# Batch 0's first x tiles normalised in pairs by head halves, and another order of block 0's first units

## The chip, the cores and the metric

The kernel runs on one core of one Trainium2 chip. The metric is the device time of one execution in microseconds, the lower the better; the median of several runs is quoted. Engines are named as in the profile: PE (TensorE, matmuls and transposes), PEld (its weight loads), DVE (VectorE), ACT (ScalarE), POOL (GpSimd), SP (SyncE, which here issues DMAs).

## What is computed

A linear attention ("cosformer") of 8 batches, 8 heads, 576 positions and head width 64, followed by a gated feed-forward block over all 4608 tokens:

```python
def phi(x, c, s):
    r = np.maximum(x, 0.0)
    return np.concatenate([r * c, r * s], axis=-1)     # 64 -> 128 features
q_p = phi(q, cos_w, sin_w); k_p = phi(k, cos_w, sin_w)
kv  = np.einsum('bhsf,bhsd->bhfd', k_p, v)
z   = np.sum(k_p, axis=2)
num = np.einsum('bhsf,bhfd->bhsd', q_p, kv)
den = np.einsum('bhsf,bhf->bhs', q_p, z)[..., None] + 1e-06
x   = (num / den)            # transposed and reshaped to (4608, 512)
out = (gelu(x @ w_gate) * (x @ w_val)) @ w_out         # 512 -> 1536 -> 512
```

Inputs and the output are float32; the matmuls take bfloat16. In the kernel gelu is the activation function of ACT.

## The kernel before

**Tiles.** A batch's 576 positions are held as four tiles of 128 and one of 64. The features are 128 per head, so `kp` and `qp` hold, for each tile `j` and head, 64 cosine and 64 sine columns; `sk` and `sq` scale k and q into them (one instruction for the cosine half and one for the sine half, `"v"` for DVE and `"s"` for ACT; a pair of last arguments restricts it to some heads). `cast_v` turns v into bfloat16 with a column of ones beside it, so that the matmul that gives kv gives z as well. `kv_half(b, g, ...)` makes kv of four heads (group g) in one PSUM bank, 20 matmuls, and `kv_evac` copies it to SBUF. `q_by_pe` turns a q tile by eight PE transposes into a bank, and `q_evac` copies it into `qT`. `numer_mm(b, t, bank, g)` makes numerators and denominators of tile t and group g in bank `bank + g`; `norm` takes the reciprocal of den and multiplies (three DVE instructions) into `xb`; `x_by_pe` turns that by four PE transposes, one for each 128 channels, and copies them into `xT`, which the feed-forward block reads. `numer` is both groups of `numer_mm` and one `norm` over both.

**Feed-forward block.** The hidden width 1536 is cut into 12 tiles `jt`. `gate(n, jt, c0, w, gb)` is four matmuls into bank `gb` for `w` token columns from `c0` of block n, and a gelu by ACT into one of four `gel` buffers. `value` is four matmuls into another bank and, by DVE, the product with `gel` into `hT`. `gv_unit` is a gate and its value. Block 0 has 576 columns, the later ones 512.

**Order.** The kernel fixes the order of every engine's instructions by the order of the program text (`tc.manual_schedule()`); each engine runs its own list in that order and waits on semaphores for what the other engines make. At the start k, q and v of batch 0 come by DMA from SP's and ACT's queues, v in two halves of heads; the weights come by POOL's queue, the first of them (`load_w(0, 2)`) behind a copy by ACT that reads q, the last of batch 0 (`load_w(8, 12)`) behind a small POOL copy that reads x of tile 0, so that the loads follow each other. `dummies(n)` are matmuls whose result nobody reads. q of batch 1 and the weights `wo` follow on POOL behind the last scales of q; k and v of batch 1 wait for the first part of `wo`.

Block 0's first units are written out by hand. As soon as the x^T columns of tile t are there (128 columns, 64 for tile 4), gates and values over these columns can run. In the text before, tile 0's columns are used by weight tiles 0 and 1, then tile 1's, then weight tiles 2 and 3 over both (`A`, 256 columns), and so on; `X(t, bank, eng)` stands for the transposes and copy of tile t, `Y(t, bank)` for its numerators and norm. From weight tile 4's second part on (`Bw`, 320 columns) a loop carries on, then the blocks follow; the change does not touch them.

Of the kernel before, what the change touches and what calls it, by code (L numbers as in the profile page):

```python
# [9 lines left out]
FP32 = mybir.dt.float32  # L10
BF16 = mybir.dt.bfloat16
AF = mybir.ActivationFunctionType
ALU = mybir.AluOpType
# [3 lines left out]
def kernel(  # L17
# [10 lines left out]
    nc = tc.nc  # L28

    B, H, S, D = q.shape  # L30
# [4 lines left out]
    CT = C // 128  # L35
    JT = J // 128
    NJ = 4
    EPS = 1e-6
# [11 lines left out]
    rot = ctx.enter_context(tc.tile_pool(name="rot", bufs=2))  # L50
    pp = ctx.enter_context(tc.tile_pool(name="pp", bufs=1, space=bass.MemoryType.PSUM))

    ps = pp.tile([128, 8, 512], FP32, name="ps")
# [15 lines left out]
    hT = [sb.tile([128, JT, 64 + 576], BF16, name=f"hT{i}") for i in range(2)]  # L69

    junk = hT[1][:, 0, 0:512]
    ident = sb.tile([128, 128], BF16, name="ident")
    tiny = sb.tile([1, 8], FP32, name="tiny")

# [50 lines left out]
    def dummies(n, bank=7):  # L125
        for _ in range(n):
            nc.tensor.matmul(ps[:, bank, :], lhsT=junk[:, 0:128], rhs=junk, start=True, stop=True)  # L127
# [20 lines left out]
        )  # L148


    def kv_half(b, g, bank, eng="s"):
        for h in range(4 * g, 4 * g + 4):
            for j in range(NJ + 1):
                nc.tensor.matmul(  # L154
                    ps[:, bank, (h % 4) * (D + 1):(h % 4 + 1) * (D + 1)],
                    lhsT=kp[:, j, h, :],
                    rhs=vx[b % 2][:, j, h, 0:D + 1],
                    start=(j == 0), stop=(j == NJ),
                )
        if eng is not None:  # L160
            kv_evac(b, g, bank, eng)

    def kv_evac(b, g, bank, eng):
        src = ps[:, bank, 0:4 * (D + 1)].rearrange("p (h e) -> p h e", e=D + 1)
        dst = kv[b % 2][:, 4 * g:4 * g + 4, 0:D + 1]
        (nc.scalar.copy if eng == "s" else nc.vector.tensor_copy)(dst, src)

    def numer_mm(b, t, bank, g, rows=128):
        for h in range(4 * g, 4 * g + 4):
            nc.tensor.matmul(  # L170
                ps[0:rows, bank + g, (h % 4) * (D + 1):(h % 4 + 1) * (D + 1)],
                lhsT=qT[b % 2][:, t, h, 0:rows],
                rhs=kv[b % 2][:, h, 0:D + 1],
                start=True, stop=True,
            )

    def norm(xb, bank, g0, g1, rows=128):

        n = g1 - g0
        nd = ps[0:rows, bank + g0:bank + g1, 0:4 * (D + 1)].rearrange("p g (h e) -> p g h e", e=D + 1)  # L180
        den = rot.tile([128, 2, 4], FP32, name="den")
        nc.vector.tensor_scalar(den[0:rows, 0:n], nd[:, :, :, D], EPS, None, op0=ALU.add)  # L182
        rec = rot.tile([128, 2, 4], FP32, name="rec")
        nc.vector.reciprocal(rec[0:rows, 0:n], den[0:rows, 0:n])
        nc.vector.tensor_tensor(  # L185
            xb[0:rows, g0:g1], nd[:, :, :, 0:D],
            rec[0:rows, 0:n, :, None].to_broadcast([rows, n, 4, D]), op=ALU.mult,
        )

    def new_xb():  # L190
        return rot.tile([128, 2, 4, D], BF16, name="xb", bufs=4)

# [21 lines left out]
    def gate(n, jt, c0, w, gb):  # L214

        p0 = starts[n] + c0
        for ct in range(CT):
            nc.tensor.matmul(  # L218
                ps[:, gb, 0:w], lhsT=wg_sb[:, ct, jt * 128:(jt + 1) * 128],
                rhs=xT[:, ct, p0:p0 + w], start=(ct == 0), stop=(ct == CT - 1),  # L220
            )
        gels[n, jt, c0] = gel = rot.tile([128, 512], FP32, name="gel", bufs=4)
        nc.scalar.activation(gel[:, 0:w], ps[:, gb, 0:w], AF.Gelu)  # L223

    def value(n, jt, c0, w, vb):

        p0 = starts[n] + c0
        for ct in range(CT):
            nc.tensor.matmul(  # L229
                ps[:, vb, 0:w], lhsT=wv_sb[:, ct, jt * 128:(jt + 1) * 128],  # L230
                rhs=xT[:, ct, p0:p0 + w], start=(ct == 0), stop=(ct == CT - 1),
            )
        gel = gels.pop((n, jt, c0))
        nc.vector.tensor_mul(hT[n % 2][:, jt, 64 + c0:64 + c0 + w], gel[:, 0:w], ps[:, vb, 0:w])  # L234

    def gv_unit(n, jt, c0, w, gb, vb, mid=()):
        gate(n, jt, c0, w, gb)
        for f in mid:
            f()
        value(n, jt, c0, w, vb)  # L240
# [79 lines left out]
    def q_by_pe(b, j, bank, eng, h0=0, h1=H):  # L320

        qb = ps[:, bank, :].bitcast(BF16).rearrange("p (h t) -> p h t", h=H)
        for h in range(h0, h1):
            nc.tensor.transpose(out=qb[:, h, :], in_=qp[:, j, h, :], identity=ident)  # L324
        if eng is not None:
            q_evac(b, j, bank, eng, h0, h1)

    def q_evac(b, j, bank, eng, h0=0, h1=H):
        qb = ps[:, bank, :].bitcast(BF16).rearrange("p (h t) -> p h t", h=H)
        cp = nc.vector.tensor_copy if eng == "v" else nc.scalar.copy  # L330
        if j < NJ:
            cp(qT[b % 2][:, j, h0:h1], qb[:, h0:h1])
        else:
            cp(qT[b % 2][:, j, h0:h1, 0:64], qb[:, h0:h1, 0:128:2])

    def x_by_pe(b, t, xb, bank, eng, c0=0, c1=CT):
        p0 = b * S + t * 128
        cp = nc.vector.tensor_copy if eng == "v" else nc.scalar.copy
        xb2 = xb.rearrange("p g h d -> p (g h d)")
        rows = 128 if t < NJ else 64  # L340
        view = ps[:, bank, 0:256].bitcast(BF16).rearrange("p (c t) -> p c t", c=CT)
        for ct in range(c0, c1):
            nc.tensor.transpose(  # L343
                out=view[:, ct, 0:rows], in_=xb2[0:rows, ct * 128:(ct + 1) * 128], identity=ident[0:rows, 0:rows],
            )
        cp(xT[:, c0:c1, p0:p0 + rows], view[:, c0:c1, 0:rows])  # L346

    def sq(j, which, eng, *h):
        scale(Q, j, which, eng, *h)

    def sk(j, which, eng, *h):
        scale(K, j, which, eng, *h)
# [3 lines left out]
    for h0 in (0, 4):  # L356
        for j in range(NJ + 1):
            sk(j, 0, "v", h0, h0 + 4)
            sk(j, 1, "v" if j < 2 else "s", h0, h0 + 4)
    nc.scalar.copy(wg_sb[0:2, 0, 0:1], qf[0:2, 7, 1, D - 1:D])  # L360
    load_w(0, 2)
    load_w(2, 4)
    load_w(4, 8)
    for j in range(2):
        sq(j, 0, "v"), sq(j, 1, "s")
        q_by_pe(0, j, j, None)
    dummies(3)
    q_evac(0, 0, 0, "v")
    cast_v(0, 0, 2, "v")
    cast_v(0, 2, 4, "s")  # L370
    kv_half(0, 0, 4, None)
    q_evac(0, 1, 1, "v")
    dummies(2)
    cast_v(0, 4, 6, "v")
    cast_v(0, 6, 8, "s")
    kv_evac(0, 0, 4, "v")
    kv_half(0, 1, 5, "s")
    x0, x1 = new_xb(), new_xb()
    numer_mm(0, 0, 6, 0)
    norm(x0, 6, 0, 1)  # L380
    dummies(1, 4)
    numer_mm(0, 0, 6, 1)
    sq(2, 1, "s")
    norm(x0, 6, 1, 2)
    sq(2, 0, "v")
    numer_mm(0, 1, 0, 0)
    numer_mm(0, 1, 0, 1)
    norm(x1, 0, 0, 2)
    x_by_pe(0, 0, x0, 4, "s", 0, 2)
    dummies(2, 5)  # L390
    x_by_pe(0, 0, x0, 4, "s", 2, 4)
    q_by_pe(0, 2, 3, None)

    nc.gpsimd.tensor_copy(tiny[0:1, 1:2], x0[0:1, 1, 3, D - 1:D])
    load_w(8, 12)


    A, Bw = (0, 256), (256, 320)
    xs = {1: x1}

    def X(t, bank, eng):
        return lambda: x_by_pe(0, t, xs[t], bank, eng)

    def Y(t, bank):
        def f():
            xs[t] = numer(0, t, bank, 128 if t < NJ else 64)
        return f

    gate(0, 0, 0, 128, 5)
    gate(0, 1, 0, 128, 4)  # L410
    X(1, 2, "s")()
    q_evac(0, 2, 3, "v")
    sq(3, 0, "v"), sq(3, 1, "s")
    value(0, 0, 0, 128, 6)
    value(0, 1, 0, 128, 7)
    Y(2, 0)()
    gate(0, 0, 128, 128, 5)
    gate(0, 1, 128, 128, 4)
    value(0, 0, 128, 128, 2)
    value(0, 1, 128, 128, 3)  # L420
    q_by_pe(0, 3, 6, "s")
    gate(0, 2, *A, 5)
    X(2, 0, "v")()
    sq(4, 1, "s"), sq(4, 0, "v")
    gate(0, 3, *A, 4)
    value(0, 2, *A, 7)
    Y(3, 0)()
    value(0, 3, *A, 2)
    q_by_pe(0, 4, 3, "s")
    gv_unit(0, 0, 256, 128, 5, 6)  # L430
    gv_unit(0, 1, 256, 128, 4, 7, (X(3, 0, "s"),))
    Y(4, 2)()
    gv_unit(0, 0, 384, 128, 5, 1)
    gv_unit(0, 1, 384, 128, 4, 0)
    gate(0, 4, *A, 5)
    X(4, 7, "v")()
    gate(0, 5, *A, 4)
    gv_unit(0, 2, *Bw, 2, 6)
    gv_unit(0, 3, *Bw, 3, 7)
    value(0, 4, *A, 1)  # L440
    value(0, 5, *A, 2)
    gv_unit(0, 0, 512, 64, 4, 6)
    gv_unit(0, 1, 512, 64, 5, 7)


    load_q(1, nc.gpsimd)
# [23 lines left out]
    for jt in range(4, 12):  # L470
        for i, (c0, w) in enumerate((A, Bw)):
            if (jt, i) not in ((4, 0), (5, 0)):
                j = 0 if jt == 4 else i
# [59 lines left out]
    for n in range(1, 7):  # L533
        b = n + 1
# [5 lines left out]
        s = 0 if n > 1 else -1  # L540
# [70 lines left out]
```

## Time and profile before

| | |
|---|---|
| median of 3 runs | 325.84 us (325.72 to 325.84) |
| the profiled execution | 326.12 us, of which the span from the first to the last instruction is 324.3 us |
| PE busy | 315.1 us, 97% |
| DVE, ACT, POOL busy | 168.0, 151.3, 21.7 us |
| first numerators of batch 0 | 14.07 us from the start of the span |
| first gate of block 0 | 16.88 us |
| first gate of the loop after the hand-written units | 29.88 us |

Times in the text are microseconds from the start of the span. In a timeline row the first number is the start, the second how long the merged instructions took together, then the engine, the line, the operation, what it writes and reads, shapes, and the count; in brackets stands the idle time of the engine before it and what ended it. [...]

### The profile page before, as it was taken

How to read it: one execution, taken by the hardware profiler on the slowest of the kernel's cores; microseconds unless marked ns; L12 is line 12 of the kernel's file. 1: busy time of each engine (PE TensorE's matmuls, PEld its weight loads, DVE VectorE, ACT ScalarE, POOL GpSimd, SP SyncE). 2: the span in 40 equal slices, each digit the busy share in tenths (PEclk: the TensorE clock that was granted, in tenths of full speed). 3: DMA queues.
4: the chain of work that ended last, by engine and by line, in shares of the span. 5: the costliest groups of instructions: out<-in, count | busy, mean ns of one | idle time of the engine just before them, and what ended most of it. 6: DMA issues, size and time to landing. Idle time of an engine off the chain costs nothing.

```text
span 324.3 us, 5829 instructions
## 1 busy us (share of the span) xinstructions
PE 315.1 (97%) x2185; PEld 167.1 (52%) x2218; DVE 168.0 (52%) x380; ACT 151.3 (47%) x271; POOL 21.7 (7%) x43
## 2 busy tenths in 40 slices
PE   7899999999999999999999999999999999999994
PEld 3587866455445544544455445544554444444443
DVE  4885776677564576366636574647454222222210
ACT  5674764853583248325642565237522222323321
POOL 2551000001100010001000100010000100100000
PEclk9999999999999999999999999999999999999999
DMA  7999999999899939991999289936333111000124
GB/s 223 287 204 275 226 307 306 324 200 172 282 222 345 219 51 194 333 236 51 195 324 242 50 153 294 301 68 124 104 73 75 32 32 34 32 32 32 37 63 98
DMA packets 88300, 55.56 MB, mean 171 GB/s; under 512 B 53072, under 2 KB 83536, under 8 KB 88272
## 3 DMA queue, kind: packets, MB, share of 16 engines
q1 hardware_dynamic: 81744, 48.84, 60.8%
q0 software_dynamic: 6096, 5.90, 10.2%
q10 hardware_dynamic: 432, 0.46, 0.4%
q8 instruction: 17, 0.28, 0.3%
q14 instruction: 11, 0.09, 0.1%
HBM read 37.75 MB, written 9.44 MB: 146 GB/s over the span
## 4 chain that ended last, share of the span: by engine, by line
PE 93%; DMA 2%; SPq 1%; DVE 1%; issue 1%; POOL 0%; ACT 0%; POOLq 0%; DVEq 0%
PE ps L218 29%; PE ps L229 29%; PE ps L259 28%; PE ps L170 3%; PE ps L154 3%; DMA vf<-in_v_dram 2%; SPq L80 1%; PE ps L277 1%; PE ps L324 1%; PE ps L343 1%; DVE vx L141 0%; ACT xT L346 0%; DVE qp L135 0%; POOL vf L98 0%; POOL qf L97 0%
## 5 line engine op out<-in xcount | busy, mean ns | idle before, releaser
L234 DVE TENSOR_TENSOR hT<-gel,ps 128x512 bf16<-128x512 f32 (+5 forms) x126 | 76.1, 607 | 89.3 <-PE ps L229 88.4
L218 PE MATMUL ps<-xT,wg_sb 128*128 128x512 bf16 (+5 forms) x492 | 111.8, 348 | 0.7
L229 PE MATMUL ps<-xT,wv_sb 128*128 128x512 bf16 (+5 forms) x496 | 111.8, 348 | 0.4
L223 ACT ACTIVATE gel<-ps 128x512 f32<-128x512 f32 (+5 forms) x126 | 67.4, 536 | 74.2 <-PE ps L218 51.9
L259 PE MATMUL ps<-wo_sb,hT 128*128 128x512 bf16 x408 | 94.3, 379 | 0.6
L218 PEld LDWEIGHTS <-wg_sb 128*128 128x128 bf16 x504 | 47.1, 98 | 44.5
L229 PEld LDWEIGHTS <-wv_sb 128*128 128x128 bf16 x504 | 45.7, 98 | 39.0
L259 PEld LDWEIGHTS <-hT 128*128 128x128 bf16 x420 | 40.8, 98 | 47.7
L288 ACT COPY o_sb<-ps 128x512 f32<-128x512 f32 x35 | 20.5, 586 | 76.2 <-PE ps L259 69.9
L185 DVE TENSOR_TENSOR xb<-ps,rec 128x512 bf16<-128x512 f32 (+2 forms) x41 | 27.8, 678 | 2.8 <-DMA xr<-xb 1.4
L182 DVE TENSOR_SCALAR den<-ps 128x8 f32<-128x8 f32 (+2 forms) x41 | 6.7, 163 | 42.2 <-PE ps L170 42.2
L137 ACT ACTIVATE kp<-kf,sin_c 128x512 bf16<-128x512 f32 (+1 forms) x41 | 25.4, 681 | 0.8 <-DMA kf<-in_k_dram 0.8
L170 PEld LDWEIGHTS <-qT 128*128 128x128 bf16 (+1 forms) x320 | 15.1, 98 | 8.3 <-issue 0.4
L137 ACT ACTIVATE qp<-qf,sin_c 128x512 bf16<-128x512 f32 x28 | 19.3, 713 | 0.1
L135 DVE TENSOR_SCALAR kp<-kf,cos_c 128x512 bf16<-128x512 f32 (+1 forms) x45 | 18.1, 450 | 1.4 <-DMA kf<-in_k_dram 1.4
L135 DVE TENSOR_SCALAR qp<-qf,cos_c 128x512 bf16<-128x512 f32 x40 | 18.2, 495 | 0.0
L209 POOL COPY xT<-xr 128x256 bf16<-128x256 bf16 x7 | 2.8, 402 | 208.7 <-DMA xr<-xb 208.7
L170 PE MATMUL ps<-kv,qT 128*128 128x65 bf16 (+1 forms) x320 | 16.6, 194 | 0.1
L154 PEld LDWEIGHTS <-kp 128*128 128x128 bf16 x320 | 10.9, 97 | 2.6 <-issue 0.7
L127 PE MATMUL ps<-hT 128*128 128x512 bf16 x33 | 10.2, 460 | 1.8 <-DVE par_i L104 1.7
L154 PE MATMUL ps<-vx,kp 128*128 128x65 bf16 x320 | 11.2, 193 | 0.1
L141 ACT CAST vx<-vf 128x1280 bf16<-128x1280 f32 (+1 forms) x9 | 9.7, 1076 | 1.2 <-DMA vf<-in_v_dram 1.2
(54 smaller groups left out, 88.6 us busy)
## 6 DMA issues: line engine op xcount, KB each, us to landing
out_dram<-o_sb SPq DMA_DIRECT2D x38, 128.0 KB, 2.4
kf<-in_k_dram SPq DMA_DIRECT2D x7, 640.0 KB, 7.3
out_dram<-o_sb SPq DMA_DIRECT2D x16, 256.0 KB, 2.9
qf<-in_q_dram SPq DMA_DIRECT2D x6, 640.0 KB, 6.2
vf<-in_v_dram SPq DMA_DIRECT2D x6, 640.0 KB, 8.7
kf<-in_k_dram SPq DMA_DIRECT2D x7, 512.0 KB, 6.2
qf<-in_q_dram SPq DMA_DIRECT2D x6, 512.0 KB, 4.9
vf<-in_v_dram SPq DMA_DIRECT2D x6, 512.0 KB, 7.8
```

Of the source, the lines that this page charges most:

```text
L127: nc.tensor.matmul(ps[:, bank, :], lhsT=junk[:, 0:128], rhs=junk, start=True, stop=True)
L135: nc.vector.tensor_scalar(d, s, col, 0.0, op0=ALU.mult, op1=ALU.max)
L137: nc.scalar.activation(d, s, AF.Relu, scale=col)
L154: nc.tensor.matmul(ps[:, bank, (h % 4) * (D + 1):(h % 4 + 1) * (D + 1)], lhsT=kp[:, j, h, :], rhs=vx[b % 2][:, j, h, 0:D + 1], start=(j == ...
L170: nc.tensor.matmul(ps[0:rows, bank + g, (h % 4) * (D + 1):(h % 4 + 1) * (D + 1)], lhsT=qT[b % 2][:, t, h, 0:rows], rhs=kv[b % 2][:, h, 0:D ...
L185: nc.vector.tensor_tensor(xb[0:rows, g0:g1], nd[:, :, :, 0:D], rec[0:rows, 0:n, :, None].to_broadcast([rows, n, 4, D]), op=ALU.mult,)
L218: nc.tensor.matmul(ps[:, gb, 0:w], lhsT=wg_sb[:, ct, jt * 128:(jt + 1) * 128], rhs=xT[:, ct, p0:p0 + w], start=(ct == 0), stop=(ct == CT - 1),
L223: nc.scalar.activation(gel[:, 0:w], ps[:, gb, 0:w], AF.Gelu)
L229: nc.tensor.matmul(ps[:, vb, 0:w], lhsT=wv_sb[:, ct, jt * 128:(jt + 1) * 128], rhs=xT[:, ct, p0:p0 + w], start=(ct == 0), stop=(ct == CT - 1),
L234: nc.vector.tensor_mul(hT[n % 2][:, jt, 64 + c0:64 + c0 + w], gel[:, 0:w], ps[:, vb, 0:w])
L259: nc.tensor.matmul(ps[:, bank, :], lhsT=hT[n % 2][:, jt, c0:c0 + 128], rhs=wo_sb[:, jt, :], start=(jt == 0), stop=(jt == JT - 1),)
L288: nc.scalar.copy(o_sb, ps[:, bank, :])
```

## The change

It has five parts.

1. Scales and casts. In the second half of k's heads, the sine scale of position tile 1 goes from DVE to ACT. Of q tile 0's sine scale, heads 4 to 7 go from ACT to DVE. The copy of kv of group 0 goes from DVE to ACT, and stands there ahead of ACT's cast of v's heads 6 and 7. `kv_half` of group 0 takes its heads in the order 2, 3, 0, 1.
2. Numerators of group 0 of tiles 0 and 1 stand side by side in banks 6 and 7, ahead of `kv_half` of group 1, and are normalised together by a new `norm_pair`; those of group 1 follow in banks 0 and 1, and there `norm_pair` multiplies one tile at a time. It writes into `xp`, a part of `hT[1]` that is free then.
3. x of tile 0 and tile 1 is turned in halves of two transposes each; the first half of tile 0 is copied by DVE, the others by ACT.
4. Dummies before the q copies are two instead of three, and others are moved.
5. Block 0's first units have another order and other banks: q tile 2 is turned after the first gates, gates of 128 columns of weight tiles 0 and 1 are taken with those of other tiles, two values have their products separated (`product`) and put behind the copy of tile 2, tile 3's copy goes from ACT to DVE behind three products, and the units around tile 4 are exchanged.

```diff
     junk = hT[1][:, 0, 0:512]
+    xp = hT[1][:, 1:3, 0:512].rearrange("p t (g h d) -> p t g h d", g=2, h=4)
...
-    def kv_half(b, g, bank, eng="s"):
-        for h in range(4 * g, 4 * g + 4):
+    def kv_half(b, g, bank, eng="s", heads=None):
+        for h in heads or range(4 * g, 4 * g + 4):
...
+    def norm_pair(bank, g, n):
+
+        nd = ps[:, bank:bank + 2, 0:4 * (D + 1)].rearrange("p t (h e) -> p t h e", e=D + 1)
+        den = rot.tile([128, 2, 4], FP32, name="den")
+        nc.vector.tensor_scalar(den, nd[:, :, :, D], EPS, None, op0=ALU.add)
+        rec = rot.tile([128, 2, 4], FP32, name="rec")
+        nc.vector.reciprocal(rec, den)
+        for t in range(0, 2, n):
+            nc.vector.tensor_tensor(
+                xp[:, t:t + n, g], nd[:, t:t + n, :, 0:D],
+                rec[:, t:t + n, :, None].to_broadcast([128, n, 4, D]), op=ALU.mult,
+            )
...
-            sk(j, 1, "v" if j < 2 else "s", h0, h0 + 4)
+            sk(j, 1, "v" if j < (2 if h0 == 0 else 1) else "s", h0, h0 + 4)
...
-    for j in range(2):
-        sq(j, 0, "v"), sq(j, 1, "s")
-        q_by_pe(0, j, j, None)
-    dummies(3)
+    sq(0, 0, "v"), sq(0, 1, "s", 0, 4), sq(0, 1, "v", 4, 8)
+    q_by_pe(0, 0, 0, None)
+    sq(1, 0, "v"), sq(1, 1, "s")
+    q_by_pe(0, 1, 1, None)
+    dummies(2)
     q_evac(0, 0, 0, "v")
     cast_v(0, 0, 2, "v")
     cast_v(0, 2, 4, "s")
-    kv_half(0, 0, 4, None)
+    kv_half(0, 0, 4, "s", (2, 3, 0, 1))
     q_evac(0, 1, 1, "v")
     dummies(2)
     cast_v(0, 4, 6, "v")
     cast_v(0, 6, 8, "s")
-    kv_evac(0, 0, 4, "v")
+
+    numer_mm(0, 0, 6, 0)
+    numer_mm(0, 1, 7, 0)
     kv_half(0, 1, 5, "s")
-    x0, x1 = new_xb(), new_xb()
-    numer_mm(0, 0, 6, 0)
-    norm(x0, 6, 0, 1)
-    dummies(1, 4)
-    numer_mm(0, 0, 6, 1)
+    norm_pair(6, 0, 2)
+    dummies(1, 3)
+    x_by_pe(0, 0, xp[:, 0], 4, "v", 0, 2)
+    numer_mm(0, 0, -1, 1)
+    numer_mm(0, 1, 0, 1)
+    norm_pair(0, 1, 1)
     sq(2, 1, "s")
-    norm(x0, 6, 1, 2)
-    sq(2, 0, "v")
-    numer_mm(0, 1, 0, 0)
-    numer_mm(0, 1, 0, 1)
-    norm(x1, 0, 0, 2)
-    x_by_pe(0, 0, x0, 4, "s", 0, 2)
-    dummies(2, 5)
-    x_by_pe(0, 0, x0, 4, "s", 2, 4)
-    q_by_pe(0, 2, 3, None)
-
-    nc.gpsimd.tensor_copy(tiny[0:1, 1:2], x0[0:1, 1, 3, D - 1:D])
+    x_by_pe(0, 1, xp[:, 1], 2, "s", 0, 2)
+    dummies(3, 3)
+    x_by_pe(0, 0, xp[:, 0], 4, "s", 2, 4)
+    sq(2, 0, "v"), sq(3, 0, "v")
+    x_by_pe(0, 1, xp[:, 1], 2, "s", 2, 4)
+
+    nc.gpsimd.tensor_copy(tiny[0:1, 1:2], xp[0:1, 0, 1, 3, D - 1:D])
     load_w(8, 12)
...
     gate(0, 0, 0, 128, 5)
-    gate(0, 1, 0, 128, 4)
-    X(1, 2, "s")()
-    q_evac(0, 2, 3, "v")
-    sq(3, 0, "v"), sq(3, 1, "s")
-    value(0, 0, 0, 128, 6)
-    value(0, 1, 0, 128, 7)
-    Y(2, 0)()
-    gate(0, 0, 128, 128, 5)
+    gate(0, 1, 0, 128, 6)
+    sq(3, 1, "s")
+    q_by_pe(0, 2, 3, "v")
+    gate(0, 0, 128, 128, 7)
     gate(0, 1, 128, 128, 4)
-    value(0, 0, 128, 128, 2)
-    value(0, 1, 128, 128, 3)
-    q_by_pe(0, 3, 6, "s")
-    gate(0, 2, *A, 5)
-    X(2, 0, "v")()
+    value(0, 0, 0, 128, 0)
+    value(0, 1, 0, 128, 1)
+    Y(2, 2)()
+    value(0, 0, 128, 128, 5, False)
+    value(0, 1, 128, 128, 6, False)
+    q_by_pe(0, 3, 7, "s")
+    gate(0, 2, *A, 4)
+    X(2, 2, "v")()
+    product(0, 0, 128, 128, 5)
+    product(0, 1, 128, 128, 6)
     sq(4, 1, "s"), sq(4, 0, "v")
-    gate(0, 3, *A, 4)
-    value(0, 2, *A, 7)
-    Y(3, 0)()
-    value(0, 3, *A, 2)
-    q_by_pe(0, 4, 3, "s")
-    gv_unit(0, 0, 256, 128, 5, 6)
-    gv_unit(0, 1, 256, 128, 4, 7, (X(3, 0, "s"),))
-    Y(4, 2)()
-    gv_unit(0, 0, 384, 128, 5, 1)
-    gv_unit(0, 1, 384, 128, 4, 0)
-    gate(0, 4, *A, 5)
-    X(4, 7, "v")()
-    gate(0, 5, *A, 4)
-    gv_unit(0, 2, *Bw, 2, 6)
-    gv_unit(0, 3, *Bw, 3, 7)
-    value(0, 4, *A, 1)
+    gate(0, 3, *A, 3)
+    gate(0, 0, 256, 128, 0)
+    gate(0, 1, 256, 128, 1)
+    value(0, 2, *A, 2)
+    Y(3, 6)()
+    value(0, 3, *A, 5)
+    value(0, 0, 256, 128, 4)
+    value(0, 1, 256, 128, 3)
+    q_by_pe(0, 4, 0, "s")
+    X(3, 6, "v")()
+    gate(0, 4, *A, 1)
+    gate(0, 0, 384, 128, 2)
+    value(0, 0, 384, 128, 5)
+    Y(4, 6)()
+    gv_unit(0, 1, 384, 128, 3, 4)
+    gate(0, 5, *A, 0)
+    X(4, 6, "v")()
+    value(0, 4, *A, 7)
     value(0, 5, *A, 2)
-    gv_unit(0, 0, 512, 64, 4, 6)
-    gv_unit(0, 1, 512, 64, 5, 7)
+    gv_unit(0, 2, *Bw, 1, 5)
+    gv_unit(0, 3, *Bw, 3, 4)
+    gv_unit(0, 0, 512, 64, 0, 6)
+    gv_unit(0, 1, 512, 64, 1, 3)
```

`value` got a last argument `now=True`; with `False` it leaves its DVE product to a later call of `product`. `x_by_pe` and its copy were cut in two in the same way (`x_evac`).

More of the change, by code (lines that the diff above doesn't have):

```diff
@@ L223, in gate, with value @@
         nc.scalar.activation(gel[:, 0:w], ps[:, gb, 0:w], AF.Gelu)
-    def value(n, jt, c0, w, vb):
+    def value(n, jt, c0, w, vb, now=True):
         p0 = starts[n] + c0
@@ L232, in value, with product @@
             )
+        if now:
+            product(n, jt, c0, w, vb)
+    def product(n, jt, c0, w, vb):
         gel = gels.pop((n, jt, c0))
@@ L336, in x_by_pe @@
     def x_by_pe(b, t, xb, bank, eng, c0=0, c1=CT):
-        p0 = b * S + t * 128
-        cp = nc.vector.tensor_copy if eng == "v" else nc.scalar.copy
         xb2 = xb.rearrange("p g h d -> p (g h d)")
@@ L345, in x_by_pe, with x_evac @@
             )
+        if eng is not None:
+            x_evac(b, t, bank, eng, c0, c1)
+    def x_evac(b, t, bank, eng, c0=0, c1=CT):
+        p0 = b * S + t * 128
+        cp = nc.vector.tensor_copy if eng == "v" else nc.scalar.copy
+        rows = 128 if t < NJ else 64
+        view = ps[:, bank, 0:256].bitcast(BF16).rearrange("p (c t) -> p c t", c=CT)
         cp(xT[:, c0:c1, p0:p0 + rows], view[:, c0:c1, 0:rows])
@@ L375 @@
     cast_v(0, 6, 8, "s")
-    kv_evac(0, 0, 4, "v")
+    numer_mm(0, 0, 6, 0)
+    numer_mm(0, 1, 7, 0)
     kv_half(0, 1, 5, "s")
-    x0, x1 = new_xb(), new_xb()
-    numer_mm(0, 0, 6, 0)
-    norm(x0, 6, 0, 1)
-    dummies(1, 4)
-    numer_mm(0, 0, 6, 1)
-    sq(2, 1, "s")
-    norm(x0, 6, 1, 2)
-    sq(2, 0, "v")
-    numer_mm(0, 1, 0, 0)
-    numer_mm(0, 1, 0, 1)
-    norm(x1, 0, 0, 2)
-    x_by_pe(0, 0, x0, 4, "s", 0, 2)
-    dummies(2, 5)
-    x_by_pe(0, 0, x0, 4, "s", 2, 4)
-    q_by_pe(0, 2, 3, None)
-    nc.gpsimd.tensor_copy(tiny[0:1, 1:2], x0[0:1, 1, 3, D - 1:D])
+    norm_pair(6, 0, 2)
[4 more added lines that the diff above has]
+    norm_pair(0, 1, 1)
+    sq(2, 1, "s")
+    x_by_pe(0, 1, xp[:, 1], 2, "s", 0, 2)
[4 more added lines that the diff above has]
+    nc.gpsimd.tensor_copy(tiny[0:1, 1:2], xp[0:1, 0, 1, 3, D - 1:D])
     load_w(8, 12)
     A, Bw = (0, 256), (256, 320)
-    xs = {1: x1}
+    xs = {}
     def X(t, bank, eng):
```

## The prediction
> **What bounds it.** I read the page's busy shares, then its chain that ended last, then the windows of TensorE (PE), then the timelines of single stretches.
>
> ```profile
> PE 315.1 (97%) x2185; PEld 167.1 (52%) x2218; DVE 168.0 (52%) x380; ACT 151.3 (47%) x271; POOL 21.7 (7%) x43
> PE 93%; DMA 2%; SPq 1%; DVE 1%; issue 1%; POOL 0%; ACT 0%; POOLq 0%; DVEq 0%
> ```
>
> PE carries 93% of the last chain, so what counts is when PE gets through its list, not how busy VectorE (DVE) or ScalarE (ACT) is. The windows say where PE has room:
>
> ```profile
> 17.00:22.00 5.00, 5.00 (x81) 1.00 1.32 205
> 26.00:30.00 4.00, 4.00 (x45) 1.00 1.19 270
> 30.00:45.00 15.00, 15.00 (x131) 1.00 1.15 286
> ```
>
> Columns: stretch, length, PE busy, clock, DMA. After 30 us PE is full, and no wait of PE is listed from there to the end. So block 0's first units, which end at 29.88 (the next 128x320 gate starts there), decide: a microsecond won or lost by then is won or lost at the end. The edit lies wholly before that point.
>
> The chain runs over v's second half (landed 12.71), its cast (to 13.44), kv_half (13.48 to 14.24), numerators, norm, transposes, and the first gate at 16.88. After it, PE is nearly dense:
>
> ```profile
> 16.42 0.62 PE L324 MATMUL ps<-ident,qp 128*128 128x128 bf16 x8
> 16.88 0.61 PE L218 MATMUL ps<-xT,wg_sb 128*128 128x128 bf16 x8
> 17.46 0.40 PE L343 MATMUL ps<-ident,xb 128*128 128x128 bf16 x4
> ...
> 20.30 0.39 PE L343 MATMUL ps<-ident,xb 128*128 128x128 bf16 x4
> 20.53 0.60 PE L218 MATMUL ps<-xT,wg_sb 128*128 128x256 bf16 x4
> ```
>
> A busy figure includes the tail of the last matmul; the step to the next start is the true cost: 8 transposes 0.44, 4 of them 0.22, a gate or value of 128 columns 0.22, of 256 0.44, of 320 0.54; likewise 8 numerators 0.26. Counting all PE work from 17.32 (gates done) to 29.88 with these steps gives 11.78 us; 12.56 passed. The kernel before loses 0.78 there.
>
> The price of a tile's x is in the VectorE rows:
>
> ```profile
> 18.71 0.16 DVE L182 TENSOR_SCALAR den<-ps 128x8 f32<-128x8 f32 x1
> 18.90 0.20 DVE L184 RECIPROCAL rec<-den 128x8 f32<-128x8 f32 x1
> 19.14 0.69 DVE L185 TENSOR_TENSOR xb<-ps,rec 128x512 bf16<-128x512 f32 x1
> 20.73 0.42 DVE L346 COPY xT<-ps 128x512 bf16<-128x512 bf16 x1 [0.51 <-PE ps L343]
> ```
>
> From numerators to usable x^T: numerators start, den 0.46 later (18.14 + 0.42 + 0.04), rec 0.20, multiply 0.24, its length 0.69, 0.06 to PE: 1.65 to the transposes. Then 0.43 (20.30 to 20.73) + 0.42 + 0.05 = 0.90 to the gate that needs it. PE has to fill 1.65 and 0.90 with other work, less the numerators (0.26) and transposes (0.22) themselves. Before does so after tile 3: its copy ends 24.22, the gate starts 24.27, a gap of 0.26.
>
> [...] the first kv weights loaded at 11.80, their matmul waited until 12.16. So a late x^T stops everything behind it. [...]
>
> **Edit by edit, the start.** On VectorE one k scale of the second half goes (6 instead of 7, 0.26 each from 7.73): free at 9.31, but q lands at 9.42, so 0.15 is won. Tile 0's sine is split: ACT does heads 0 to 3 (a 128x256 row, 0.49: 9.52 to 10.01), VectorE the rest. Transposes end earlier, and q_evac starts at about 10.71 instead of 10.95, cast_v ends 11.87 instead of 12.11, kv_half of group 0 starts 11.87 instead of 12.16. ACT takes over kv_evac: 12.67 to 13.05, and its own cast of heads 6, 7 moves behind it to 13.70; kv_half reaches those heads at 13.78, so that costs nothing. Eight numerators of group 0 start 13.10, before v's second half is used: den 13.56 (before: 14.40), multiply of 512 elements 14.00 to 14.69.
>
> That lead is lost on group 1, which still hangs on v: kv_half 13.48 to 14.24, kv_evac to 14.66, as before. Tile 0's first transposes stand ahead of its numerators and wait for 14.69: 14.75. Numerators 14.86 (before 14.71), den 15.32 (before 15.15), multiplies 15.76 to 16.18 and 16.10 to 16.52 (two of 256 at 0.42, step 0.34). Tile 0's second transposes 16.24, ACT's copy 0.32 later, 16.56 to 16.93 (before ended 16.72). Gate 0's first two matmuls run from 16.69, the others from 16.98; both gates are through at 17.31. Before: 17.32. **The start gains nothing**; and before has by then turned q of tile 2 (0.44) where after has turned x of tile 1 (0.22). Work left: 11.78 + 0.22 = 12.00.
>
> Fewer and moved dummies lie in PE idle time: nothing[...]. POOL's load_w of columns 8 to 11 hangs on 16.18 instead of 15.97: lands 0.2 later, about 28; first used after 32. q's loads for batch 1 wait on tile 3 and 4 scales, the second 22.0 as before; wo and SP's k and v follow unchanged. Weights needed earlier have landed: wg 4 to 7 issued 13.00 + 9.4 = 22.4, now used at 24.13; wv 4 to 7 at 24.94, used at 27.49.
>
> **The units' order.** From 17.31, PE steps as above:
> q tile 2 to 17.75, copy on VectorE 17.96 to 18.64 (0.65 after the first transpose, as 19.42 to 20.07, and a 0.68 row); gates and values to 18.63; numerators of tile 2 at 18.69, stall 0.06.
> den 19.15, multiply to 20.28; PE is there at 20.27; X at 20.34, stall 0.07.
> Copy 20.77 to 21.19. Only gate(0,3), 0.44, stands between: 0.90 - 0.22 - 0.44, stall 0.24. Gates of columns 256 from 21.24.
> value(0,2) 21.68, its product 22.38 (0.70 later, as 32.49 to 33.19), then den 22.72, multiply to 23.85; PE is free 23.70, X of tile 3 at 23.91, stall 0.21.
> Its copy is now on VectorE behind three products (23.77, 24.11, 24.33): 24.55 to 24.97. PE has only gate(0,4): stall 0.45, of which 0.24 would stay if VectorE were free. Gate of columns 384 at 25.02.
> Numerators of tile 4, 64 rows wide: 0.10 to switch in and out each (before: 23.65 to 23.75, 25.60 to 25.70). den 26.04, multiply to 27.21; PE has two units of 0.22 and gate(0,5): X at 27.27, stall 0.47. Before put 1.32 of gates and values there.
> Stalls: 0.06 + 0.07 + 0.24 + 0.21 + 0.45 + 0.20 + 0.47 = 1.70. End: 17.31 + 12.00 + 1.70 = 31.01 against 29.88: **1.1 us later**. gel's four buffers and the banks come free in time everywhere I looked (tightest: product(0,1) at 19.1 for gate(0,3)'s gel at 21.9).
>
> All operations have rows in the trace; unsure are the joins. Below: the start 0.2 earlier, VectorE's queue ahead of X of tile 3 not there (0.21) and no switching loss (0.20) leave +0.5. Above: the start 0.2 later and two more queueings of 0.1 give +1.5. The profiled execution took 326.12 for a span of 324.3; 327.2 is forecast for such a one. The median is 0.28 lower, 325.84; so 326.9.
>
> **Rivals.** (1) The stalls come out small, +0.5 by the low bounds: 326.3, and not to be told from no change (0.2% is 0.65 us, about what a measurement can tell). For: three stalls are under 0.22. Against: those of 0.24, 0.24 and 0.47 follow from PE's order alone.
> (2) Not slower: group 0's norm, 0.84 earlier, and the larger choice of gates cover the latency. With no stall the end is 29.31: 325.3. It decides at a stall sum of 0.57; the 0.95 just named speaks against it.
> (3) PE's clock falls: [...] Against: granted clock 0.999 with similar gaps before[...]. Late weights go with this.
>
> **Chances.** Forecast 0.62, small stalls 0.25, not slower 0.07, clock or weights 0.06. A not-slower case is counted as faster though full cover would give only -0.57. Slower by over 0.2%: 0.62 + 0.06 = 0.68; within: 0.25; faster: 0.07. The range of 326.2 to 327.4 runs from a little below the low bound to the high one; it leaves out rivals 2 and 3.
>
> **What will show it.** den of group 0 near 13.6, first gate near 16.7 with a break, x copies of tiles 2 and 3 ending near 21.2 and 25.0 with PE idle before the next gate, transposes of tile 4 near 27.3, first 128x320 gate of weight tile 4 near 31.0. Gates through by 16.9, or that gate by 29.9, would make the forecast wrong.

## The result, and the profile after

The changed kernel takes **327.12 us** (median; 326.81 to 327.33) against 325.81 (325.72 to 325.93) for the kernel before on the same chip: 1.31 us more, ratio 1.0039 with a 95% interval of 1.0025 to 1.0053. One of its six executions, the profiled one, ran at a granted clock of 0.559 and took 560.45 us; it counts in that median (327.10 without it) but not in the ratio, and the rows below come from a second profile of the same kernel (label `after_again`: 327.40 us for a span of 325.5; in that comparison 327.38 against 325.80, ratio 1.0045, interval 1.0033 to 1.0058).

From the page of that profile, the busy shares and the chain that ended last:

```profile
PE 317.5 (98%) x2218; PEld 166.9 (51%) x2218; DVE 168.3 (52%) x379; ACT 150.9 (46%) x272; POOL 22.0 (7%) x43
...
PE 92%; DVE 2%; DMA 2%; issue 1%; SPq 1%; ACT 1%; POOL 0%; DVEq 0%; ACTq 0%; POOLq 0%
```

Nothing here tells of a slower kernel. PE's busy time went up by 2.4 us, but its instructions in the page went from 2185 to 2218: the trace of before missed a few matmul records (PEld, the weight loads, has 2218 in both pages). PE carries 92% instead of 93%, DVE 2% instead of 1%. The loss shows only in a list of PE's waits (what waited, for whom, us in total, times, longest):

```profile
PE ps L128 <- DVE par_i L105: 1.7, 1, 1.7
PE ps L359 <- DVE xb L186: 0.7, 2, 0.5
PE ps L359 <- DVE hT L199: 0.4, 2, 0.2
PE ps L342 <- ACT qp L138: 0.2, 1, 0.2
PE ps L232 <- DVE xT L370: 0.2, 1, 0.2
```

The same list of before has only the first of these and one wait of 0.6 for q's first scale. New are the waits for DVE's `xb` and `xT` inside block 0. The windows (stretch, length, PE busy, clock, DMA) put them before 30 us. The first row is of before, the others are of the changed kernel:

```profile
20.00:30.00 10.00, 9.92 (x134) 1.00 1.23 233
...
20.00:30.00 10.00, 9.03 (x111) 1.00 1.22 232
30.00:45.00 15.00, 15.00 (x143) 1.00 1.15 287
```

PE was busy 9.92 of ten microseconds before, and 9.03 after. After 30 us PE is full in both, so nothing is won back: the first matmul group of block 1 starts at 59.69 instead of 58.24, the last group of the program at 318.31 instead of 316.85. Both shifts equal that of the join, the first 128x320 gate of weight tile 4, which starts at 31.33 instead of 29.88. From the join to PE's last matmul both take 289.5 us. The span grew by only 1.2, because what follows PE's last matmul took 4.92 us in the profiled execution of before and 4.68 in this one.

The waits one by one, from PE's timeline of the changed kernel:

```profile
16.56 0.79 PE L232 MATMUL ps<-xT,wg_sb 128*128 128x128 bf16 x8
17.18 0.61 PE L342 MATMUL ps<-ident,qp 128*128 128x128 bf16 x8
...
20.46 1.28 PE L232 MATMUL ps<-xT,wg_sb 128*128 128x256 bf16 x12
...
23.16 0.61 PE L342 MATMUL ps<-ident,qp 128*128 128x128 bf16 x8
24.23 0.40 PE L359 MATMUL ps<-ident,xb 128*128 128x128 bf16 x4 [0.46 <-DVE xb L186]
24.46 0.60 PE L232 MATMUL ps<-xT,wg_sb 128*128 128x256 bf16 x4
25.29 0.38 PE L232 MATMUL ps<-xT,wg_sb 128*128 128x128 bf16 x4 [0.22 <-DVE xT L370]
...
26.66 0.60 PE L232 MATMUL ps<-xT,wg_sb 128*128 128x256 bf16 x4
27.46 0.29 PE L359 MATMUL ps<-ident,xb 64*128 64x64 bf16 x4 [0.21 <-DVE xb L186]
...
31.33 0.70 PE L232 MATMUL ps<-xT,wg_sb 128*128 128x320 bf16 x4
```

Read each row by the step to the next start, not by the bracket. Eight transposes need 0.44, so PE was free at 23.60 and tile 3's transposes came at 24.23: a stall of 0.63. The bracket says 0.46, because the length of the row of eight (0.61) reaches 0.17 beyond the 0.44 at which the next matmul can start. In the same way: 0.39 before 25.29, 0.36 before 27.46, and inside the row of twelve, which takes 1.13 to the next start (21.59) where 0.88 is work, 0.24 (by the single records). `128x320` at 31.33 comes 0.12 late as well: its bank 0 waits for the gelu of the 64-column gate just before (31.20 would be the next start; ACT's row of the two 64-column gelus begins at 31.06 and is 0.46 long). With the small ones (0.06 and 0.06 before tile 2's numerators and transposes, 0.09 and 0.12 around tile 4's numerators) they make 2.07.

DVE's timeline of the same kernel over the largest of them:

```profile
20.67 0.42 DVE L370 COPY xT<-ps 128x512 bf16<-128x512 bf16 x1 [0.49 <-PE ps L359]
21.01 0.48 DVE L252 TENSOR_TENSOR hT<-gel,ps 128x128 bf16<-128x128 f32 x2
21.40 0.48 DVE L136 TENSOR_SCALAR qp<-qf,cos_c 128x512 bf16<-128x512 f32 x1
22.72 0.42 DVE L252 TENSOR_TENSOR hT<-gel,ps 128x256 bf16<-128x256 f32 x1 [0.84 <-ACT gel L237]
23.05 0.16 DVE L183 TENSOR_SCALAR den<-ps 128x8 f32<-128x8 f32 x1
23.25 0.20 DVE L185 RECIPROCAL rec<-den 128x8 f32<-128x8 f32 x1
23.48 0.69 DVE L186 TENSOR_TENSOR xb<-ps,rec 128x512 bf16<-128x512 f32 x1
```

DVE's rows overlap like PE's: the scale at 21.40 begins 0.09 before the products' row ends (21.01 + 0.48). The order is what the text predicted: den, reciprocal and multiply of tile 3 stand behind the product of value(0, 2). But that product starts at 22.72, and its bracket misleads: the gelu it names had ended at 21.24. Value(0, 2) started at 21.59 and, by the 0.70 that the prediction took from before, should have let it go at 22.29. In the single records of the trace, where a wait for a semaphore is a record of its own, DVE's wait ends at 22.25, and the product starts 0.47 after that.

### The profile page after: what moved, and what is told of

Read it like the earlier page. It is cut to its first block, busy times and chain, and to the rows that moved or that the text cites. A ratio compares the mean times of both kernels' runs of the same rounds, so it can differ in the third digit from the quotient of the medians.

```text
span 558.5 us, 5823 instructions
## 1 busy us (share of the span) xinstructions
PE 546.1 (98%) x2185; PEld 233.6 (42%) x2218; DVE 171.8 (31%) x379; ACT 152.2 (27%) x272; POOL 21.8 (4%) x43
## 4 chain that ended last, share of the span: by engine, by line
PE 97%; issue 1%; DVE 0%; ACT 0%
PE ps L243 29%; PE ps L232 29%; PE ps L277 28%; PE ps L171 3%; PE ps L155 3%; PE ps L128 2%; PE ps L342 1%; PE ps L295 1%; PE ps L359 1%; DVE hT L199 0%; DVE qp L136 0%; ACT xT L370 0%; DVE o_sb L300 0%; ACT o_sb L299 0%; DVE hT L93 0%
## 5 line engine op out<-in xcount | busy, mean ns | idle before, releaser
L232 PE MATMUL ps<-xT,wg_sb 128*128 128x512 bf16 (+5 forms) x492 | 186.8, 526 | 2.4 <-issue 1.4
L243 PE MATMUL ps<-xT,wv_sb 128*128 128x512 bf16 (+5 forms) x496 | 186.3, 526 | 1.4 <-issue 0.7
L277 PE MATMUL ps<-wo_sb,hT 128*128 128x512 bf16 x408 | 164.4, 582 | 2.3 <-issue 1.4
L232 PEld LDWEIGHTS <-wg_sb 128*128 128x128 bf16 x504 | 63.8, 131 | 97.3 <-issue 89.8
L277 PEld LDWEIGHTS <-hT 128*128 128x128 bf16 x420 | 55.6, 133 | 101.8 <-issue 101.3
L243 PEld LDWEIGHTS <-wv_sb 128*128 128x128 bf16 x504 | 62.4, 131 | 85.3 <-issue 78.7
L171 PEld LDWEIGHTS <-qT 128*128 128x128 bf16 (+1 forms) x320 | 22.4, 121 | 17.4 <-issue 17.2
L186 DVE TENSOR_TENSOR xb<-ps,rec 128x512 bf16<-128x512 f32 (+1 forms) x38 | 26.3, 691 | 1.3
L171 PE MATMUL ps<-kv,qT 128*128 128x65 bf16 (+1 forms) x320 | 23.6, 232 | 0.0
L138 ACT ACTIVATE qp<-qf,sin_c 128x512 bf16<-128x512 f32 (+1 forms) x28 | 19.0, 705 | 0.0
```

The source lines that it names most:

```text
L138: nc.scalar.activation(d, s, AF.Relu, scale=col)
L171: nc.tensor.matmul(ps[0:rows, bank + g, (h % 4) * (D + 1):(h % 4 + 1) * (D + 1)], lhsT=qT[b % 2][:, t, h, 0:rows], rhs=kv[b % 2][:, h, 0:D ...
L186: nc.vector.tensor_tensor(xb[0:rows, g0:g1], nd[:, :, :, 0:D], rec[0:rows, 0:n, :, None].to_broadcast([rows, n, 4, D]), op=ALU.mult,)
L232: nc.tensor.matmul(ps[:, gb, 0:w], lhsT=wg_sb[:, ct, jt * 128:(jt + 1) * 128], rhs=xT[:, ct, p0:p0 + w], start=(ct == 0), stop=(ct == CT - 1),
L243: nc.tensor.matmul(ps[:, vb, 0:w], lhsT=wv_sb[:, ct, jt * 128:(jt + 1) * 128], rhs=xT[:, ct, p0:p0 + w], start=(ct == 0), stop=(ct == CT - 1),
L277: nc.tensor.matmul(ps[:, bank, :], lhsT=hT[n % 2][:, jt, c0:c0 + 128], rhs=wo_sb[:, jt, :], start=(jt == 0), stop=(jt == JT - 1),)
```

## Experiments

Two marks are compared across all runs, since the cast of v's second half on DVE starts anywhere from 12.37 to 12.83 us. **Start** is from the start of that cast to the gate of weight tile 2, by when PE has done the same work in every kernel. **Units** is from that gate to the join. Both come from one profile of each kernel, the medians from all its executions. Ratios are to the kernel before in the same comparison: 325.80 for after_again, start_new, order_new and filled, 325.85 for after_shift, x4_fill, filled2 and start_new_gate4, 325.91 for the last four; each comparison ran on another chip. (The row of before has the median of the result.) So medians are best compared by their distance from before.

| kernel | median us | ratio (95%) | start | units |
|---|---|---|---|---|
| before | 325.81 | | 7.07 | 10.01 |
| after_again | 327.38 | 1.0045 (1.0033 to 1.0058) | 7.11 | 11.59 |
| start_new | 325.70 | 0.9994 (0.9986 to 1.0002) | 7.08 | 10.07 |
| order_new | 326.70 | 1.0029 (1.0019 to 1.0038) | 7.12 | 11.18 |
| filled | 326.67 | 1.0023 (1.0014 to 1.0032) | 7.10 | 11.41, with 0.87 of work more |
| after_shift | 326.73 | 1.0030 (1.0018 to 1.0041) | 7.13 | 11.17 |
| x4_fill | 327.16 | 1.0042 (1.0030 to 1.0055) | 7.10 | 11.30 |
| filled2 | 326.04 | 1.0007 (1.0001 to 1.0014) | 7.08 | 11.01, with 0.87 of work more |
| start_new_gate4 | 325.79 | 1.0001 (0.9993 to 1.0009) | 7.11 | 10.06 |
| gate4_copy_first | 325.66 | 0.9990 (0.9983 to 0.9996) | 7.06 | 9.94 |
| group1_first | 325.75 | 0.9993 (0.9987 to 1.0000) | 7.17 | 9.93 |
| after_pair | 327.30 | 1.0037 (1.0024 to 1.0049) | 7.11 | 11.58 |
| shift_pair | 326.81 | 1.0026 (1.0019 to 1.0032) | 7.11 | 11.18 |

The theory on trial was the prediction's: the start gains nothing, and the new order leaves PE too little to do while x of tiles 2, 3 and 4 is made. The rivals: the start is at fault, the clock or late weights, or something in VectorE that has nothing to do with the order of PE's work.

**after_again** is the changed kernel without an edit.

> The changed kernel once more, for its trace. Forecast's theory (the order of the units): first gate's first two matmuls near 16.7, both first gates through near 17.3, so the start is level with the kernel before (17.32). x copy of tile 2 ends near 21.2, of tile 3 near 25.0, transposes of tile 4 near 27.3, the first 128x320 gate of weight tile 4 near 31.0 (29.88 before): PE stalls of 0.24, 0.21, 0.45 and 0.47 in that order. About +1.1 us. Rival (the start): both first gates are through 0.5 or more later than 17.3, and the stalls after it sum to no more than the 0.78 of before. Rival (later): the gate of weight tile 4 starts within 0.3 of 29.9 and the time goes after 30 us.

Its rows are shown above. It settles that the clock (0.997) is not the cause, and brings the delay of the product to light.

**start_new and order_new** part the change at the gate of weight tile 2. The first has the changed start and units up to tile 3's q transposes, and from there the order of before (with banks that fit):

```diff
-    gate(0, 3, *A, 3), gate(0, 0, 256, 128, 0), gate(0, 1, 256, 128, 1)
-    value(0, 2, *A, 2), Y(3, 6)(), value(0, 3, *A, 5)
...
+    gate(0, 3, *A, 3), value(0, 2, *A, 5), Y(3, 0)(), value(0, 3, *A, 6)
+    q_by_pe(0, 4, 7, "s")
+    gv_unit(0, 0, 256, 128, 4, 5)
+    gv_unit(0, 1, 256, 128, 3, 2, (X(3, 0, "s"),))
...
```

> The changed start and first units, up to and with the transposes of q tile 3; from the gate of weight tile 2 on, the order of the kernel before (tile 3's copy on ScalarE, units around tile 4 as before). Order theory: that gate starts within 0.1 of the 19.87 of before, so the time is that of before, 325.8, within 0.3. Start theory: all of the loss, +1.1 to +1.3 us, near 327.0.

The other has the start of before, and the changed order from that gate on.

> The start and first units of the kernel before, up to and with the transposes of q tile 3; from the gate of weight tile 2 on, the changed order. Order theory: the stalls of 0.24, 0.21, 0.45 and 0.47 all lie in this part, so +1.1 to +1.2 us, near 327.0. Start theory: 325.8, within 0.3.

One piece of the change is in neither: both make the products of columns 128 at once, where the changed kernel puts them behind tile 2's copy. after_shift, below, has them there and its units are 11.17 against 11.18 for order_new, so this piece shows no cost of its own.

The start alone costs nothing that can be measured: 7.08 against 7.07, and 325.70 is within the noise of before. The order alone takes 11.18 where before took 10.01: 1.17 by the trace, 0.90 by the medians (the marks of single profiles come out up to 0.3 higher than the medians here). PE's windows show the same in the stretch where before has 9.92 and the changed kernel 9.03. The row of start_new:

```profile
20.00:30.00 10.00, 9.92 (x133) 1.00 1.23 235
```

And the row of order_new, with 0.54 less:

```profile
20.00:30.00 10.00, 9.38 (x114) 1.00 1.22 234
```

But PE runs the same list from that gate in order_new as in the changed kernel, and is 0.41 faster through it. PE's timeline of order_new shows where, to be held against the rows at 23.16 and 24.23 above:

```profile
23.03 0.61 PE L324 MATMUL ps<-ident,qp 128*128 128x128 bf16 x8
23.68 0.40 PE L343 MATMUL ps<-ident,xb 128*128 128x128 bf16 x4
```

Tile 3's transposes come 0.21 after PE was free (23.03 + 0.44), the very figure predicted. DVE's product of value(0, 2) starts there 0.05 after its wait ended:

```profile
22.16 0.42 DVE L234 TENSOR_TENSOR hT<-gel,ps 128x256 bf16<-128x256 f32 x1 [0.81 <-PE ps L229]
```

So 0.42 of the stall in the changed kernel belongs to VectorE, with the same list of work on PE. VectorE's own list differs by the two products of columns 128, but in the changed kernel these were done at 21.49 and the scale behind them at 21.88, before the wait ended at 22.25.

**after_shift** asks whether that delay hangs on where the product stands in VectorE's list. In the changed kernel it is the 64th record of VectorE in the trace (waits counted), in order_new the 67th. The edit is one instruction on one element, far ahead of it, that nobody waits for:

```diff
+    nc.vector.memset(tiny[0:1, 2:3], 0.0)
```

> The changed kernel with one more VectorE instruction, a memset of one element, in the first 2 us. In the trace of the changed kernel and of the filled one, the product of weight tile 2 starts 0.49 us after the wait for its value has ended, where the kernel with only the order changed takes 0.07; nothing of what it waits for is late. [...] the delay of some 0.42 belongs to the place of that instruction in VectorE's list, so one instruction ahead moves it to another instruction; tile 3's transposes start 0.4 earlier after their numerators, and the time falls by 0.2 to 0.4 us. Rival: it belongs to the buffers or banks of that product, and nothing changes (0 within 0.15).

The expectation counts from the start of the wait's record (0.49 and 0.07), the rest of this text from its end (0.47 and 0.05). Here the wait ended at 22.01 and the product started at 22.05: the delay is gone, the buffers and banks being the same, and units fell from 11.59 to 11.17. As this and the changed kernel had been timed in different comparisons, the two were run again side by side.

> The changed kernel beside the next one on the same chip, for a clean difference: 327.1 to 327.4.

> The changed kernel with one more VectorE instruction at its beginning, a second time. If the delay of 0.4 us hangs on the place in VectorE's list, 0.3 to 0.5 us below the changed kernel run beside it, and the product of weight tile 2 within 0.1 us of its wait; if the earlier run was luck, within 0.15 of it.

DVE's timeline of after_pair has the product late:

```profile
22.52 0.42 DVE L252 TENSOR_TENSOR hT<-gel,ps 128x256 bf16<-128x256 f32 x1 [0.82 <-ACT gel L237]
```

The same row in DVE's timeline of shift_pair:

```profile
22.25 0.42 DVE L253 TENSOR_TENSOR hT<-gel,ps 128x256 bf16<-128x256 f32 x1 [0.42 <-ACT gel L238]
```

The waits had ended at 22.07 and 22.20. The product is 0.45 late in the one and 0.05 in the other, PE's stall before tile 3's transposes is 0.62 and 0.21, and the kernel takes 327.30 and 326.81. An added instruction makes the kernel 0.49 faster by the medians and 0.40 by the trace. The ranges overlap only in their ends: 327.15 to 327.37 in five executions, 326.36 to 327.30 in twenty-one.

**x4_fill** puts the value of weight tile 4 ahead of tile 4's transposes, to fill one predicted stall with work of the kernel itself:

```diff
+    value(0, 4, *A, 2, False)
     X(4, 6, "v")()
-    value(0, 4, *A, 7)
-    value(0, 5, *A, 2)
+    product(0, 4, *A, 2)
+    value(0, 5, *A, 7)
```

> The changed kernel with the value of weight tile 4 ahead of tile 4's transposes (its product behind their copy). Order theory: the stall of 0.36 ahead of these transposes goes, nothing comes in its place, so -0.3 to -0.4 us against the changed kernel. Rival: PE only waits elsewhere, for tile 4's copy, and the time stays within 0.1.

In its trace the stall falls from 0.36 to 0.10 and units from 11.59 to 11.30. By time it is 1.31 above the kernel before (327.16), and the changed kernel was 1.31, 1.58 and 1.39 above it in its three comparisons. So the trace shows the stall filled, but the medians don't show the 0.3 to 0.4 that was expected.

**filled** fills all the larger stalls: value(0, 2) and tile 3's numerators go ahead of the gates of columns 256, products of that tile go behind tile 3's copy, and the gate and value of weight tile 6 (0.87 of PE work) are pulled out of the loop.

```diff
     gate(0, 3, *A, 3)
-    gate(0, 0, 256, 128, 0), gate(0, 1, 256, 128, 1)
     value(0, 2, *A, 2), Y(3, 6)()
+    gate(0, 0, 256, 128, 0), gate(0, 1, 256, 128, 1)
...
+    gate(0, 5, *A, 0)
...
+    value(0, 4, *A, 1), gate(0, 6, *A, 2)
```

> The changed kernel with PE work put where the forecast has its stalls: value of weight tile 2 and numerators of tile 3 ahead of the gates of columns 256; tile 3's copy ahead of two products on VectorE, with gates of weight tiles 4 and 5 behind its transposes; value of weight tile 4 and a gate of weight tile 6 ahead of tile 4's transposes (that unit is taken out of the loop). Same work. Order theory: of the 1.70 us of stalls some 0.35 stay, the end is 29.7 plus the unit pulled ahead, so -1.3 us against the changed kernel and -0.2 against the one before: 325.6. Start theory: no more than 0.3 us below the changed kernel.

It missed by 1.1: 326.67. PE's timeline shows a new wait at once:

```profile
20.40 0.60 PE L232 MATMUL ps<-xT,wg_sb 128*128 128x256 bf16 x4
21.08 0.60 PE L243 MATMUL ps<-xT,wv_sb 128*128 128x256 bf16 x4
```

PE was free at 20.84; value(0, 2) waited 0.24, because I had left it in bank 2, which tile 2's copy still read (20.61 to 21.03). Two units in the loop on shared banks waited 0.14 and 0.12 more, and the join 0.17. That was the experiment's own fault, not evidence on the theory, so it was mended.

**filled2** is the same with banks of their own: value(0, 2) in bank 0, the later ones shifted, and the loop's banks in turn.

> The filled kernel with its bank clashes taken away: the value of weight tile 2 in a bank that no copy holds, and the loop's units alternating banks again after the unit that was pulled ahead. Order theory: the 0.24 ahead of that value, the 0.26 in the loop and the 0.17 at its start go, so 0.6 to 0.7 us below the filled kernel, at 326.0, level with the kernel before within 0.2. Rival: the filled kernel's remainder comes from elsewhere and this is as slow, 326.5 or more.

326.04, which is 0.19 above before (ratio 1.0007, interval 1.0001 to 1.0014). Units less the 0.87 are 10.14, against 11.59 for the changed kernel and 10.01 before. PE's window and its timeline:

```profile
20.00:30.00 10.00, 9.97 (x122) 1.00 1.23 236
...
23.02 0.61 PE L342 MATMUL ps<-ident,qp 128*128 128x128 bf16 x8
23.47 0.39 PE L359 MATMUL ps<-ident,xb 128*128 128x128 bf16 x4
```

Its product of value(0, 2) is again the 64th record and again 0.46 late, but now PE has gates to run meanwhile, and tile 3's transposes come as soon as PE is free (23.02 + 0.44). A stall of 0.20 is left ahead of tile 3's numerators (21.44): their bank 6 was read until 21.38 by a product of columns 128. With the stalls filled, the slowdown is almost gone, which is the strongest support for the prediction's mechanism.

**start_new_gate4 and gate4_copy_first** look for something better than both. Before and start_new both lose 0.26 ahead of the gate of columns 384. The first edit puts a gate of 256 columns there:

```diff
     Y(4, 2)()
+    gate(0, 4, *A, 5)
     gv_unit(0, 0, 384, 128, 4, 1)
     gv_unit(0, 1, 384, 128, 3, 0)
-    gate(0, 4, *A, 5)
     X(4, 2, "v")()
```

> The kernel with the new start and the old order, and in it the gate of weight tile 4 moved between tile 4's numerators and the gate of columns 384, where the kernel before and this one lose 0.26 us waiting for tile 3's copy. Order theory: -0.26 against the same kernel without the move, about 325.45, faster than both kernels. Rival: tile 4's transposes, which lose that gate as cover, start later by the same amount and the time stays at 325.7.

Nothing was won: 325.79, units 10.06. The gap before the next unit fell from 0.26 to 0.12, which is what remains around 64-row matmuls; and 0.13 came back later, where the gate of weight tile 2's last 320 columns waited for tile 4's copy. DVE's timeline:

```profile
25.63 0.29 DVE L252 TENSOR_TENSOR hT<-gel,ps 128x128 bf16<-128x128 f32 x1 [0.16 <-ACT gel L237]
25.84 0.28 DVE L370 COPY xT<-ps 128x256 bf16<-128x256 bf16 x1
```

The copy stands behind a product that waits for its gelu. The second edit turns the two around:

```diff
-    gv_unit(0, 1, 384, 128, 3, 0)
+    gate(0, 1, 384, 128, 3)
+    value(0, 1, 384, 128, 0, False)
     X(4, 2, "v")()
+    product(0, 1, 384, 128, 0)
```

> The new start, the old order with the gate of weight tile 4 moved, and tile 4's copy on VectorE ahead of the product of weight tile 1, columns 384. In the trace of the move alone, the 0.26 became 0.12 (the switch to and from 64 rows stays) and 0.13 came back as a wait for tile 4's copy, which stood behind that product. If that is so, this one gains 0.13: from the gate of weight tile 2 to the first 128x320 gate of weight tile 4 it takes 9.94 instead of 10.06, near 325.65. Rival: the copy is not what that gate waits for, and the distance stays at 10.06.

DVE's timeline of it has the copy first:

```profile
25.98 0.29 DVE L370 COPY xT<-ps 128x256 bf16<-128x256 bf16 x1 [0.23 <-PE ps L359]
26.18 0.28 DVE L252 TENSOR_TENSOR hT<-gel,ps 128x128 bf16<-128x128 f32 x1
```

Units are 9.94 and the time is 325.66 against 325.91: ratio 0.9990, interval 0.9983 to 0.9996. It has the lowest median of all versions, 1.64 us below the changed kernel in the same comparison (327.30), and is faster than before by about a tenth of a per cent. The interval overlaps those of start_new and group1_first, so that it beats these is not shown. Start and units account for 0.08 of the 0.25 us; where the rest comes from is open. The profiled execution (326.17) isn't typical of it either.

**group1_first** tries the start once more: group 1's numerators of tiles 0 and 1 ahead of tile 0's first transposes, whose copy comes later from a bank of its own.

```diff
-    x_by_pe(0, 0, xp[:, 0], 4, "v", 0, 2)
     numer_mm(0, 0, -1, 1)
     numer_mm(0, 1, 0, 1)
+    x_by_pe(0, 0, xp[:, 0], 4, None, 0, 2)
     norm_pair(0, 1, 1)
+    x_evac(0, 0, 4, "v", 0, 2)
```

> The same, and in the start group 1's numerators ahead of tile 0's first transposes, the copy of these behind group 1's multiplies, and the second half of tile 0 in a bank of its own. Theory: group 1's chain is what the start hangs on, and in the changed kernel it stands behind the transposes and their copy for 0.07 to 0.1 us; so the first gates come 0.1 earlier counted from v's second cast, near 325.55, faster than both kernels. Rival: the first gate then waits for the late copy, and nothing is gained.

Start is 7.17 against 7.06: no gain. Group 1's den did come earlier, 2.45 after the start of v's cast instead of 2.52. But the first gate comes 3.89 after it, in gate4_copy_first 3.88. DVE's timeline of group1_first shows why:

```profile
16.00 0.28 DVE L370 COPY xT<-ps 128x256 bf16<-128x256 bf16 x1
16.20 1.11 DVE L136 TENSOR_SCALAR qp<-qf,cos_c 128x512 bf16<-128x512 f32 x2
```

The late copy ended at 16.28 and the gate came at 16.34: that is the rival. The first of the two scales, of q tile 2, now stands behind the copy and ended at 16.93, and that tile's transposes came at 16.98, 0.09 after PE was through with the gates.

## Why the prediction was right, point by point

It forecast 326.9 and a join 1.1 us later; measured were 327.12, 327.38 and 327.30, and in the trace 1.45. The mechanism held: the start gains nothing, and PE then waits for x at the places that were named. The size held with some luck in it. Without VectorE's delay the changed kernel takes 326.73 or 326.81, a little under the forecast; the delay, which was not forecast, lifts it a little over. Both lie in the stated range.

- **"The start gains nothing"**: right. Den of group 0 came at 13.41 (forecast 13.56), so the lead was there. First gate 16.56 with the break (0.79 for eight gates), gates through at 17.18 (forecast 17.31). As v's cast came 0.17 earlier in this execution, that is 0.04 later than forecast. start_new, 7.08 against 7.07, shows it apart from the rest.
- **The stall behind tile 2's copy, 0.24**: 0.24.
- **The stall ahead of tile 3's transposes, 0.21**: the mis-sized term, 0.63. The working took VectorE's product 0.70 after the start of its value; it came at 1.13. The 0.21 for the queue itself was right, as order_new and shift_pair show; 0.42 was added by a delay that no row of before shows.
- **The stall behind tile 3's copy, 0.45**: 0.39. The copy stood directly behind the products, as predicted.
- **Switching at tile 4's numerators, 0.10 each way**: 0.09 and 0.12.
- **The stall ahead of tile 4's transposes, 0.47**: 0.36.
- **The join**: 0.12 more, not forecast: bank 0 is given to a 64-column gate just before it. The prediction had looked at the banks and called them free in time; this one is not. filled2, with other banks, has no such gap.
- **The sum**: 2.07 against 1.70, the difference being 0.42 for VectorE, 0.12 for the join, less 0.17 on tiles 3 and 4. From 17.18 to 31.33 pass 14.15 us, of which 12.00 of work and 2.07 of stalls leave 0.08 that are not accounted for.

**Rivals.** Small stalls (326.3) and full cover (325.3) failed by the stalls above. The granted clock was 0.996 or more in the runs compared, and no wait for a weight is in PE's list; what a fall of the clock over one stretch costs, no run shows. The rival raised by the runs, that VectorE's delay is the cause, holds for about 0.4 of the 1.3 to 1.6; the order by itself gives 0.9 by the medians and 1.17 by the trace. In the trace the two make up the 1.58 by which units grew; by the medians of the last comparison the changed kernel is 1.39 above before, and 0.90 of it stay once the delay is gone.

## What to carry to other kernels

Where a full engine's list is fixed by hand, price every dependent step by its whole latency (here 1.65 from numerators to transposes and 0.90 from transposes to gate), and count the work that stands between, stage by stage: here the units taken earlier left too little to cover the next tile's latency (units 11.18 in order_new, 10.01 before). Ask of a filler whether its buffers are free by then. The run filled, with shared banks, waited 0.24 at once and came out 0.87 above before, filled2, with banks of their own, 0.19 above it; in start_new_gate4 the 0.14 that was gained came back as 0.13, behind a product that waited. Before an order is blamed for a few tenths, the same list should be run once shifted by an instruction: here that alone was 0.49 by the medians.

## What was unexpected in the hardware

**A delay that hangs on the place in VectorE's list.** In the changed kernel (twice), x4_fill, filled and filled2 the 64th record of VectorE, a product behind a semaphore wait, started 0.44 to 0.47 us after that wait had ended. These five profiles share VectorE's list up to it. With one instruction put ahead (twice) or in another list (order_new) the same product started 0.04 to 0.05 after it. So moving it one place took the delay away. That the 64th place is slow whatever stands there is not so: in before, order_new and group1_first tile 2's copy stands there, and it starts 0.42 to 0.43 after its transposes, as promptly as in the changed kernel (0.44), where it stands elsewhere. The mechanism isn't shown. One other thing moves with it: the first 8 KB packet of queue q14 within the span comes at 25.2 to 26.0 us in these five, and at 22.5 to 23.5 in the eight other profiles of the table (23.34 in before); the one added instruction brought it from 25.72 (after_pair) to 22.78 (shift_pair). In the five it comes after the product has ended, and no packet of q14 or q8 stands between the end of the wait and the product, so a link between the two is not shown.

**A PE cost around narrow matmuls.** Going to numerators 64 rows wide (the rows with `128*64`) cost 0.09 to 0.10 us in every profile, and going back 0.11 to 0.12 wherever no wait for a copy covered it; the numerators themselves follow each other every 0.03 us, as the wide ones do. Putting a larger gate there took away only the part that was a wait for data (0.26 became 0.12 in start_new_gate4).
